# Moving the Gram matrices of a delta rule one group sooner, from key copies of their own, in a kernel that overlaps it with two feed-forward layers

## The chip, the cores and the metric

The kernel runs on one core of one Trainium2 chip. The metric is the device time of one execution in microseconds; the time of the kernel before is the median of three runs. One further execution was recorded by the hardware profiler, and everything that is read from "the trace" below is of that one. Engines: TensorE (PE in the rows; PEld is its weight load), VectorE (DVE), ScalarE (ACT), GpSimd (POOL) and SyncE (SP), which issues the DMAs. Each executes its own instructions in order.

## What is computed

```python
for t in range(S):                       # attention: B=4, H=8, S=768, D=48
    kt, vt, bt = k_n[:, :, t], v[:, :, t], beta[:, :, t, None]
    y[:, :, t] = einsum('bhd,bhde->bhe', q[:, :, t], state)
    v_old = einsum('bhde,bhd->bhe', state, kt)
    state = state + bt[..., None] * einsum('bhd,bhe->bhde', kt, vt - v_old)
x = y as 3072 tokens x 384
h = x @ w_in;  g = h if h >= 1, 0 if h <= -1, else (h + 1)**2 / 4;  x = g @ w_out   # 384 -> 2048 -> 384
h = x @ w_in2; r = max(h, 0);                                      out = (r * r) @ w_out2
```

The keys `k_n` are normalized rows of `k`. All is float32; the kernel forms each product of the feed-forward layers from a high and a low part of both factors, three matmuls for one.

## The kernel before

**Attention.** Time is cut into 24 chunks of 32 tokens. Within a chunk the recurrence becomes a triangular system, and its matrix comes from the Gram matrix of the chunk's keys. Chunks are taken in six groups of four. For a group, `gram` (TensorE, L272) makes the products of keys with keys and queries of a chunk, and VectorE masks them into `gp` (L284). `tri` inverts the triangles of a whole group: `begin` transposes `gp` to `gm` (VectorE, L325), a preparation of some ten small instructions normalizes (L238 to L355, the last large one L354), then 30 steps of two GpSimd instructions each (L370, L376) work on `tx`, and `end` transposes `tx` back into `gp` (VectorE, L380). Only then can the first chunk of the group use it. The inversions of groups 1 to 5 run on GpSimd; that of group 0 stands at the start, on VectorE and GpSimd together.

A chunk has six steps on TensorE: `ks` (keys with state, L406), `tr` (with the inverse, L420), `qs` (queries with state, `yy`, L406), `ku` (the state's update, `sps`, L451), `pu` (L440) and `xt` (transposes the result for the feed-forward, L474). `value` scales a chunk's keys on GpSimd (L249).

**Feed-forward.** Tokens go in nine blocks of two or three chunks in the first layer (256 or 384 columns), and in eight blocks of three in the second. A block has 16 units, one for each 128 rows of the hidden layer. A unit is nine `h` matmuls into PSUM, the activation, and two units later nine `acc` matmuls (all L489). In the first layer the activation is ScalarE's `r` and `g` (L514, L515), VectorE's clamp (L516), ScalarE's square (L517), VectorE's sum (L518), then the split of `g` into high (ScalarE, L526) and low part (VectorE, L527). There is one L518 for each unit of the first layer, so units are counted below by their L518.

**Order.** Attention runs one block ahead of the feed-forward that consumes it. A table maps half-units (slots) to steps: a list `todo` for each block holds the steps of its chunks and the Grams, spread evenly over 32 slots; `at[c]` is the slot in which chunk `c` begins, `ready[c]` that of its Gram. TensorE executes in the order written; for the other engines a list scheduler picks the order from a simulated timeline, unless `issue_after` ties an instruction to another. `later` ties to the last L514 and L516 (`marks`). Keys and queries of a chunk (`kqt`) lie in a ring of six buffers, values (`kv`) in one of three; the ring of `kqt` serves later for second-layer weights (`w2r`).

Of the kernel before, what the change touches and what calls it, by code (L numbers as in the profile page):

```python
# [8 lines left out]
F32 = mybir.dt.float32  # L9
# [12 lines left out]
GROUPS = [4] * 6  # L22
# [3 lines left out]
def kernel(  # L26
# [38 lines left out]
    LENT = 28  # L65
    RG = 3
    RAW = 3
    WT, WL = 3, 4
    GB = 2
    MANY = 4  # L70
# [31 lines left out]
    def att(shape, name):  # L102
        tag = "att"
        if turn[0] is not None:
            tag = early[turn[0] % len(early)]
            turn[0] += 1
        return ps.tile(shape, F32, tag=tag, bufs=2 if tag == "att" else 1, name=name)
# [6 lines left out]
    kqt, kvt, gp, nt, xh, xl = {}, {}, {}, {}, {}, {}  # L114


    def load_kq(c, tag="kqt", bufs=6):
        if c >= NCH:
            return
        t = kqt[c] = ring.tile([P, B2, H, 2 * T], F32, tag=tag, bufs=bufs, name="kqt")  # L120
        for o in range(2):
            nc.sync.dma_start(
                t[64 * o:64 * o + D].rearrange("p b h x -> p (b h x)"), kq[c, D * o:D * (o + 1)]
            )

    def load_kv(c):
        if c >= NCH:
# [87 lines left out]
    w2r = {}  # L215

    def fetch_w2(f):
        w2r[f] = ring.tile([P, 2, DM], F32, tag="kqt", bufs=6, name="w2r")
        nc.sync.dma_start(w2r[f], w2f[f])

    def place_w2(f):
# [33 lines left out]
    def per_bh(f):  # L255
        for h in range(H):
            for b in range(B):
                f(b, h, slice(T * b, T * (b + 1)), slice(64 * (b % 2), 64 * (b % 2) + D))

    def gram(c, lo=0, hi=2, late=0):  # L260


        n, j = group_of[c]
        if j == 0 and lo == 0:
            gp[n] = ring.tile([P, 2, GC, H, T], F32, tag="gp", bufs=2, name="gp")
            if GROUPS[n] < GC:
                nc.gpsimd.memset(gp[n][:, 0, GROUPS[n]:], 0.0)
        g = att([P, H, hi - lo, T], "g")

        def one_(b, h, p, pd):  # L270
            x = kqt[c][pd, b // 2, h]
            nc.tensor.matmul(  # L272
                g[p, h].rearrange("p x i -> p (x i)"), x[:, 0:T], x[:, lo * T:hi * T],
                start=h == 0, stop=True, skip_group_check=True,
            )

        per_bh(one_)

        dst = gp[n][:, lo:hi, j].rearrange("p x h i -> p h x i")
        if late > 1:  # L280
            nc.scalar.copy(dst, g)

        def keep():
            nc.vector.tensor_mul(  # L284
                dst,
                dst if late > 1 else g,
                mask[:, lo:hi].rearrange("p (o x) i -> p o x i", o=1)
                .to_broadcast([P, H, hi - lo, T]),
            )

        if late:
            return keep
        keep()
# [97 lines left out]
    def chunk_steps(c):  # L391
# [38 lines left out]
        def qs():  # L430
            o = t["o"] = att([P, H, D], "yy")
            of_state(o, 1)
            if c >= HEADS:
                kqt.pop(c)
                load_kq(c + 6)

        def pu():
            o = t["o"]
# [163 lines left out]
    w1f = flow(w1s)  # L602
    w1f.reverse()

    PACE = 6
    SPREAD = 3
    behind = [nullcontext]

# [6 lines left out]
    with tc.manual_schedule():  # L615
        for c in range(GC):
            load_kq(c)
        nc.sync.dma_start(bet, beta)
        first1()
        load_kq(4)  # L620
        load_kq(5)
        for c in range(3):
            load_kv(c)
        nc.gpsimd.memset(zero, 0.0)
        nc.gpsimd.memset(one, 1.0)
        nc.gpsimd.memset(tiny, 1e-36)
        nc.gpsimd.memset(neg1, -1.0)
        nc.scalar.activation(st[:, 0, 0, 0:1], one, AF.Sqrt, bias=zero)
        nc.gpsimd.memset(mask, 1.0)
        nc.gpsimd.memset(tx, 0.0)  # L630
        for b in range(B):
            for o, op in enumerate((ALU.is_ge, ALU.is_gt)):
                m_ = mask[T * b:T * (b + 1), o]
                nc.gpsimd.affine_select(
                    m_, m_, pattern=[[1, T]], compare_op=op, fill=0.0,
                    base=0, channel_multiplier=-1,
                )
        make_identity(nc, ident)
        for c in range(GROUPS[0]):
            gram(c, 0, 1)  # L640
        begin, pre, steps, end = tri(0, [(V, 0, 3), (V, 3, 9), (G, 9, T)])
        begin()
        go(pre[:1])
        masks = [gram(0, 1, 2, late=2)]
        cross_gram(0, 1)
        go(pre[1:])
        more_w1()
        masks += [gram(c, 1, 2, late=2) for c in range(1, GROUPS[0])]
        for c in range(HEADS):
            load_kq(c + 6)  # L650
        late = masks[HEADS:]
        masks[HEADS:] = [gram(c, late=1) for c in range(GFIRST[1], GFIRST[2])]
        go(steps)
        for c in range(3):
            value(c)
        ins = end()
        go(masks)
        behind[0] = lambda: tc.issue_after(ins.ins)
    ENGINES = {mybir.EngineType.PE}
    with tc.manual_schedule(engines=ENGINES):  # L660
# [15 lines left out]
        begin()  # L676
        go(pre)
        go(t1)
        end1()
        turn[0] = None  # L680

        SL = 2 * NF
# [2 lines left out]
        def put(n, slot, *fs):  # L685
            for i, f in enumerate(fs):
                exb.setdefault(SL * n + slot + i, []).append(f)

        def later(*fs):

            def one_(f):
                with tc.issue_after(marks[0].ins), tc.issue_after(marks[1].ins):
                    f()

            return [lambda f=f: one_(f) for f in fs]

        def put_a(n, slot, f):
            exa.setdefault(SL * n + slot, []).append(f)

        at, ready, due = {}, {}, [GFIRST[2]]
        for n in range(1, NB):
            todo = []
            for c in range(FIRST[n], FIRST[n] + SIZES[n]):
                left = {0: 1, 1: 1, 2: 0, 3: 2}[c % GC]
                for i, s_ in enumerate(chunk_steps(c)):
                    todo.append(((at, c) if i == 0 else None, s_))
                    x = due[0]
                    if i + left > 5 and x < NCH:  # L710
                        left -= 1
                        due[0] += 1
                        todo.append(((ready, x), lambda x=x: gram(x)))
            for i, (mark, s_) in enumerate(todo):
                o = 0 if n > 1 else HEAD
                slot = SL * (n - 1) + o + i * (SL - o) // len(todo)
                if mark:
                    mark[0][mark[1]] = slot
                put_a(0, slot, s_)
        for c in range(3, NCH):  # L720
            put(0, max(0, at[c] - 5), lambda c=c: value(c))

        def tri_put(g, a, z):
            begin, pre, steps, end = tri(g, [(G, 0, T)])
            begin()
            for i, s_ in enumerate(pre):
                put(0, a + i // 3, s_)
            a += 4
            for i, s_ in enumerate(steps):
                put(0, a + i * min(z - a, PACE) // len(steps), s_)  # L730
            put(0, z, end)

        for g in range(2, NG):
            a, z = ready[GFIRST[g] + GROUPS[g] - 1], at[GFIRST[g]]
# [99 lines left out]
```

## Time and profile before

| what | value |
|---|---|
| median of three runs | 1101.67 us (1101.43 to 1104.24) |
| the profiled execution | 1103.17 us |
| its span in the trace | 1101.1 us |
| TensorE busy | 995.3 us, 90% of the span |
| VectorE, ScalarE, GpSimd busy | 609.3, 506.4, 293.1 us |
| mean granted clock of TensorE | 0.963 of full |

The span is the time between the first and the last instruction that the profiler recorded; what lies around it is 2.1 us in this execution. A busy share says little where matmuls are pipelined; gaps and waits say more. The first layer ends at about 700 us of the span.

### The profile page before, as it was taken

To read this page: it belongs to the slowest core of one execution; us is meant where nothing else is said; L and a number is where in the kernel's file an instruction comes from. 1 tells how busy PE (TensorE), PEld (TensorE's weight loads), DVE (VectorE), ACT (ScalarE), POOL (GpSimd) and SP (SyncE) were. 2 spreads that over 40 slices of the span, in tenths; PEclk is the share of its full clock that TensorE was granted. 3 is DMA by queue.
4 is the path that set the end of the run, shared out by engine and by line. 5 is a ranking of instruction groups with operands and counts; after the bars stand their busy time and mean duration, and the time that the engine had idled before them with its cause. 6 is when DMAs were issued, how large, how long until landed. Compare 5 with 4: busy or idle time off the path is not lost.

```text
span 1101.1 us, 32911 instructions
## 1 busy us (share of the span) xinstructions
PE 995.3 (90%) x14312; PEld 952.0 (86%) x14312; DVE 609.3 (55%) x1187; ACT 506.4 (46%) x1068; POOL 293.1 (27%) x446
## 2 busy tenths in 40 slices
PE   4345799969997997999799999899999999999998
PEld 3335699969986997899699999899999999999998
DVE  4998566754764583557644467744434343434333
ACT  1065466535544653555455666433333333333332
POOL 3467600850391058007600022310101010101000
PEclk9966899989998999899899999999999999999999
DMA  8065145223331340231211122201001010000000
GB/s 235 33 209 165 35 131 158 82 80 88 89 103 52 96 132 30 81 118 31 74 31 52 32 87 87 72 1 44 22 23 43 1 43 1 22 1 22 1 22 22
DMA packets 33488, 72.99 MB, mean 66 GB/s; under 512 B 3904, under 2 KB 17728, under 8 KB 33344
## 3 DMA queue, kind: packets, MB, share of 16 engines
q1 hardware_dynamic: 33344, 70.89, 20.9%
q8 instruction: 112, 1.84, 0.7%
q14 instruction: 32, 0.26, 0.1%
HBM read 55.15 MB, written 15.73 MB: 64 GB/s over the span
## 4 chain that ended last, share of the span: by engine, by line
PE 64%; POOL 15%; DVE 11%; issue 4%; ACT 3%; DMA 1%; SPq 0%; DVEq 0%; POOLq 0%; ACTq 0%
PE h L489 29%; PE acc L489 29%; POOL tx L376 7%; POOL t L370 7%; DVE g L518 1%; PE g L272 1%; DVE t L370 1%; DVE tx L376 1%; DVE wl L161 1%; PE tr L420 1%; PE yy L406 1%; DVE wl L164 1%; PE ks L406 1%; PE yy L440 1%; PE sps L451 1%
## 5 line engine op out<-in xcount | busy, mean ns | idle before, releaser
L489 PE MATMUL h<-xh,w 128*128 128x384 f32 (+1 forms) x1632 | 325.8, 336 | 31.3 <-ACT g L515 28.2
L489 PEld LDWEIGHTS h<-xh,w 128*128 128x128 f32 x1632 | 276.7, 193 | 37.5 <-ACT g L515 27.8
L527 DVE TENSOR_TENSOR gl<-g,gh 128x384 fp32r<-128x384 f32 (+1 forms) x272 | 167.2, 615 | 133.3 <-ACT gh L526 128.5
L526 ACT CAST gh<-g 128x384 fp32r<-128x384 f32 (+1 forms) x272 | 134.5, 494 | 209.7 <-DVE g L518 107.8
L489 PE MATMUL h<-xl,w 128*128 128x384 f32 (+1 forms) x816 | 181.3, 331 | 0.0
L489 PE MATMUL acc<-gh,w 128*128 128x384 f32 (+1 forms) x864 | 170.3, 333 | 7.2 <-ACT gh L526 6.5
L521 DVE TENSOR_TENSOR g<-r 128x384 f32<-128x384 f32 x128 | 71.3, 557 | 157.7 <-ACT r L520 157.7
L489 PE MATMUL acc<-w,gh 128*128 128x384 f32 x768 | 155.6, 337 | 1.6 <-DVE e L534 1.6
L520 ACT ACTIVATE r<-h,zero 128x384 f32<-128x384 f32 x128 | 74.5, 582 | 166.4 <-PE h L489 166.4
L489 PEld LDWEIGHTS acc<-gh,w 128*128 128x128 f32 x864 | 139.1, 193 | 12.7 <-ACT gh L526 6.6
L489 PEld LDWEIGHTS h<-xl,w 128*128 128x128 f32 x816 | 143.4, 193 | 0.0
L489 PEld LDWEIGHTS acc<-w,gh 128*128 128x128 f32 x768 | 136.3, 188 | 1.9 <-ACT gh L526 1.9
L514 ACT ACTIVATE r<-h,one 128x384 f32<-128x384 f32 (+1 forms) x144 | 78.4, 544 | 84.7 <-PE h L489 83.2
L518 DVE TENSOR_TENSOR g<-g,r 128x384 f32<-128x384 f32 (+1 forms) x144 | 89.0, 618 | 39.5 <-ACT r L517 38.2
L516 DVE TENSOR_SCALAR r<-r 128x384 f32<-128x384 f32 (+1 forms) x144 | 60.4, 419 | 84.9 <-ACT r L514 84.7
L376 POOL TENSOR_TENSOR tx<-tx,t 128x30 f32<-128x30 f32 (+16 forms) x171 | 95.5, 559 | 12.8
L370 POOL TENSOR_TENSOR t<-tx,gm 128x30 f32<-128x30 f32 (+16 forms) x171 | 92.7, 542 | 17.2 <-DVE tx L354 4.7
L489 PE MATMUL acc<-gl,w 128*128 128x384 f32 (+1 forms) x432 | 91.9, 322 | 2.3 <-DVE gl L527 2.3
L517 ACT ACTIVATE r<-r 128x384 f32<-128x384 f32 (+1 forms) x144 | 70.5, 490 | 49.5 <-DVE r L516 48.7
L249 POOL TENSOR_TENSOR kv<-kv,nt 128x384 f32<-128x384 f32 x24 | 21.7, 905 | 267.7 <-DMA kv<-in_kv_dram 73.2
L489 PE MATMUL acc<-w,gl 128*128 128x384 f32 x384 | 88.0, 337 | 0.0
L576 POOL CAST xh<-x2r 128x1152 fp32r<-128x1152 f32 x8 | 9.5, 1187 | 293.2 <-PE h L489 293.2
(85 smaller groups left out, 968.6 us busy)
## 6 DMA issues: line engine op xcount, KB each, us to landing
raw<-in_w_dram SPq DMA_DIRECT2D x64, 384.0 KB, 3.7
kqt<-in_kq_dram SPq DMA_DIRECT2D x48, 192.0 KB, 3.8
kv<-in_kv_dram SPq DMA_DIRECT2D x24, 384.0 KB, 3.1
w2f<-wl SPq DMA_DIRECT2D x32, 192.0 KB, 3.6
w2r<-w2f SPq DMA_DIRECT2D x16, 384.0 KB, 3.0
x2r<-x SPq DMA_DIRECT2D x8, 576.0 KB, 4.2
out_dram<-e SPq DMA_DIRECT2D x24, 192.0 KB, 1.9
x<-e SPq DMA_DIRECT2D x18, 192.0 KB, 3.4
```

The lines of the kernel that those rows point to most:

```text
L370: eng.tensor_mul(t, x[:, lo:hi, j:j + 1].to_broadcast([P, hi - lo, w]), gm[:, j:j + 1, j + 1:T].to_broadcast([P, hi - lo, w]),)
L376: ins = eng.tensor_add(x[:, lo:hi, j + 1:T], x[:, lo:hi, j + 1:T], t)
L406: per_bh(lambda b, h, p, pd: nc.tensor.matmul(o[p, h], kqt[c][pd, b // 2, h, x * T:(x + 1) * T], st[pd, b // 2, h], start=h == 0, stop=x = ...
L489: nc.tensor.matmul(o, *((r, l) if swap else (l, r)), **flags)
L514: marks[0] = nc.scalar.activation(r, h, AF.Relu, bias=one)
L516: marks[1] = nc.vector.tensor_scalar(r, r, 2.0, 0.5, ALU.min, ALU.mult)
L517: nc.scalar.activation(r, r, AF.Square)
L518: nc.vector.tensor_add(g, g, r)
L520: marks[0] = nc.scalar.activation(r, h, AF.Relu, bias=zero)
L521: marks[1] = nc.vector.tensor_mul(g, r, r)
L526: nc.scalar.copy(ghi, g)
L527: nc.vector.tensor_sub(glo, g, ghi.bitcast(F32))
```

## The change

Five edits go together. The keys and queries are loaded a second time for the Grams of chunks 4 to 23, into a ring of their own with two buffers (`kqg`); the ring `kqt` shrinks from six buffers to four. The four Grams of a group are all put into the first chunk of the group before it, one behind each of its steps 1 to 4, where they were spread over its last three chunks and the next group's first. The 30 inversion steps are spread over the slots up to four before the group is needed, where they were put into at most six slots. The transposition back of groups 2 to 5 is put one slot sooner and goes through `later`. That of group 1, which stood right behind its steps before the units began, is put two slots ahead of chunk 4, also through `later`.

```diff
+    KQ, KG = 4, 2
...
+    def load_kg(c):
+        if c < NCH and c not in kqg:
+            kqg[c] = fetch_kq(c, "kqg", KG)
...
-        w2r[f] = ring.tile([P, 2, DM], F32, tag="kqt", bufs=6, name="w2r")
+        w2r[f] = ring.tile([P, 2, DM], F32, tag="kqt", bufs=KQ, name="w2r")
...
+        src = kqt[c] if c < KQ else kqg[c]
...
         per_bh(one_)
+        if c >= KQ:
+            kqg.pop(c)
+            load_kg(c + KG)
...
                 kqt.pop(c)
-                load_kq(c + 6)
+                load_kq(c + KQ)
...
-        load_kq(4)
-        load_kq(5)
+        for c in range(KG):
+            load_kg(KQ + c)
...
         go(t1)
-        end1()
         turn[0] = None
...
-                left = {0: 1, 1: 1, 2: 0, 3: 2}[c % GC]
+                g, j = group_of[c]
+                due = []
+                if j == 0 and 1 <= g < NG - 1:
+                    due = list(range(GFIRST[g + 1], GFIRST[g + 1] + GROUPS[g + 1]))
                 for i, s_ in enumerate(chunk_steps(c)):
                     todo.append(((at, c) if i == 0 else None, s_))
-                    x = due[0]
-                    if i + left > 5 and x < NCH:
-                        left -= 1
-                        due[0] += 1
+                    if i and due:
+                        x = due.pop(0)
                         todo.append(((ready, x), lambda x=x: gram(x)))
...
+        put(0, at[GFIRST[1]] - 2, *later(end1))
...
-            a += 4
+            a += 3
             for i, s_ in enumerate(steps):
-                put(0, a + i * min(z - a, PACE) // len(steps), s_)
-            put(0, z, end)
+                put(0, a + i * (z - 4 - a) // len(steps), s_)
+            put(0, z - 1, *later(end))
```

What this makes of VectorE's order is shown at three places. In the changed kernel the same instructions stand on other lines: L516, L518 and L527 are L531, L533 and L542; L284, L325 and L380 are L299, L340 and L395; L477 and L416 are L492 and L431; L161 and L164 are L172 and L175.

The first place is where group 2 begins: the mask of its last Gram and the transposition of `gp`. On VectorE before, from the 27th unit sum on:

```order
L518 TENSOR_TENSOR g<-g,r 128x256
L284 TENSOR_TENSOR gp<-g,mask 128x8x2x32
L325 STREAM_TRANSPOSE gm<-gp 128x32x32
L527 TENSOR_TENSOR gl<-g,gh 128x256
L516 TENSOR_SCALAR r<-r 128x256
```

On VectorE of the changed kernel, from the 22nd unit sum on:

```order
L533 TENSOR_TENSOR g<-g,r 128x256
L542 TENSOR_TENSOR gl<-g,gh 128x256
L299 TENSOR_TENSOR gp<-g,mask 128x8x2x32
L340 STREAM_TRANSPOSE gm<-gp 128x32x32
L531 TENSOR_SCALAR r<-r 128x256
```

The beginning of group 2 moved five units to the front (groups 3, 4 and 5 likewise, by 5 to 6 units). L354 moved from just behind the 29th sum to just ahead of the 25th.

The second place is where group 2 ends: the transposition back. On VectorE before, from the 36th unit sum to the next:

```order
L518 TENSOR_TENSOR g<-g,r 128x384
L284 TENSOR_TENSOR gp<-g,mask 128x8x2x32
L527 TENSOR_TENSOR gl<-g,gh 128x384
L516 TENSOR_SCALAR r<-r 128x384
L161 TENSOR_SCALAR wl<-raw 128x384
L164 SCALAR_TENSOR_TENSOR wl<-wt,wl 128x384
L477 TENSOR_TENSOR xl<-xt,xh 128x3x128
L380 STREAM_TRANSPOSE gp<-tx 128x32x32
L518 TENSOR_TENSOR g<-g,r 128x384
```

On VectorE of the changed kernel, from the 35th unit sum to the next:

```order
L533 TENSOR_TENSOR g<-g,r 128x384
L542 TENSOR_TENSOR gl<-g,gh 128x384
L531 TENSOR_SCALAR r<-r 128x384
L395 STREAM_TRANSPOSE gp<-tx 128x32x32
L533 TENSOR_TENSOR g<-g,r 128x384
```

The transposition moved one unit to the front, and stands directly behind the clamp of a unit. The other groups' transpositions stand behind the 56th, 78th and 100th sum before, and behind the 56th, 79th and 103rd now; L354 stood behind the 49th, 70th and 92nd, and stands behind the 44th, 65th and 88th.

The third place is the transposition back of group 1. On VectorE before, from the 8th unit sum to the next:

```order
L518 TENSOR_TENSOR g<-g,r 128x256
L527 TENSOR_TENSOR gl<-g,gh 128x256
L380 STREAM_TRANSPOSE gp<-tx 128x32x32
L516 TENSOR_SCALAR r<-r 128x256
L477 TENSOR_TENSOR xl<-xt,xh 128x3x128
L518 TENSOR_TENSOR g<-g,r 128x256
```

On VectorE of the changed kernel, from the 15th unit sum to the next:

```order
L533 TENSOR_TENSOR g<-g,r 128x256
L542 TENSOR_TENSOR gl<-g,gh 128x256
L531 TENSOR_SCALAR r<-r 128x256
L395 STREAM_TRANSPOSE gp<-tx 128x32x32
L492 TENSOR_TENSOR xl<-xt,xh 128x3x128
L533 TENSOR_TENSOR g<-g,r 128x256
```

It moved seven units to the back, and from ahead of a unit's clamp to behind it.

## Rows read from the trace of the kernel before

**Rows 1.** The page: TensorE's busy time, and its granted clock in 40 slices.

```profile
PE 995.3 (90%) x14312; PEld 952.0 (86%) x14312; DVE 609.3 (55%) x1187; ACT 506.4 (46%) x1068; POOL 293.1 (27%) x446
...
PEclk9966899989998999899899999999999999999999
```

**Rows 2.** The list of waits: who waited for whom, total us, times, longest.

```profile
DVE gp L380 <- POOL tx L376: 40.0, 5, 9.7
...
PE h L489 <- ACT g L515: 28.2, 7, 8.4
...
PE tr L420 <- DVE gp L380: 12.1, 1, 12.1
```

**Rows 3.** Timeline of TensorE at its five restarts: start, us, [idle before, releaser].

```profile
131.20 1.65 PE L489 MATMUL h<-xh,w 128*128 128x256 f32 x6 [6.99 <-ACT g L515]
...
240.78 2.29 PE L489 MATMUL h<-xh,w 128*128 128x384 f32 x6 [8.36 <-ACT g L515]
...
337.86 1.93 PE L272 MATMUL g<-kqt 48*32 48x64 f32 x64 [7.65 <-DVE gp L284]
...
442.40 1.93 PE L272 MATMUL g<-kqt 48*32 48x64 f32 x64 [7.69 <-DVE gp L284]
...
548.63 2.29 PE L489 MATMUL h<-xh,w 128*128 128x384 f32 x6 [6.43 <-ACT g L515]
```

**Rows 4.** Chain of waits, 180 to 250 us (group 2): start, us, what.

```profile
187.22 1.03 PE g L272 x64
...
197.42 0.69 DVE tx L354
198.18 0.38 POOL t L370
...
212.47 0.79 POOL kv L249
...
236.94 0.27 POOL tx L376
...
240.78 3.25 PE h L489 x9
...
245.75 0.81 PE tr L420 x64
246.56 1.76 PE h L489 x9
```

**Rows 5.** Chain of waits behind the gaps of groups 4 and 5.

```profile
444.33 3.18 PE acc L489 x9
447.50 2.32 PE h L489 x9
...
551.88 2.88 PE acc L489 x9
```

**Rows 6.** Timeline of VectorE: the 25th and 36th L518, three transpositions back.

```profile
182.50 0.42 DVE L518 TENSOR_TENSOR g<-g,r 128x256 f32<-128x256 f32 x1
...
224.12 1.04 DVE L518 TENSOR_TENSOR g<-g,r 128x384 f32<-128x384 f32 x1 [0.59 <-ACT r L517]
...
237.23 2.06 DVE L380 STREAM_TRANSPOSE gp<-tx 128x1024 f32<-128x1024 f32 x1 [7.83 <-POOL tx L376]
...
334.71 2.01 DVE L380 STREAM_TRANSPOSE gp<-tx 128x1024 f32<-128x1024 f32 x1 [9.65 <-POOL tx L376]
...
543.65 2.00 DVE L380 STREAM_TRANSPOSE gp<-tx 128x1024 f32<-128x1024 f32 x1 [6.44 <-POOL tx L376]
```

**Rows 7.** Chain of waits: the 18th step from the end, groups 3 and 5.

```profile
325.60 0.59 POOL t L370
...
534.09 0.59 POOL t L370
```

**Rows 8.** Busy time by engine: PE, PEld, DVE, ACT, POOL, then clock, DMA, GB/s.

```profile
130.00:140.00 10.00, 8.80 (x224) 8.13 (x228) 8.66 (x20) 7.59 (x21) 2.33 (x3) 0.75 0.31 99
```

**Rows 9.** DMA issues: KB each, median us from issue to landing.

```profile
kqt<-in_kq_dram SPq DMA_DIRECT2D x48, 192.0 KB, 3.8
```

More of the change, by code (lines that the diff above doesn't have):

```diff
@@ L114, with load_kq, fetch_kq @@
     kqt, kvt, gp, nt, xh, xl = {}, {}, {}, {}, {}, {}
[L117 to L120, printed above, removed]
+    def load_kq(c):
+        if c < NCH:
+            kqt[c] = fetch_kq(c, "kqt", KQ)
+    kqg = {}
+    def load_kg(c):
+        if c < NCH and c not in kqg:
+            kqg[c] = fetch_kq(c, "kqg", KG)
+    def fetch_kq(c, tag, bufs):
+        t = ring.tile([P, B2, H, 2 * T], F32, tag=tag, bufs=bufs, name="kqt")
         for o in range(2):
@@ L124, in load_kq @@
             )
+        return t
     def load_kv(c):
@@ L268, in gram @@
         g = att([P, H, hi - lo, T], "g")
+        src = kqt[c] if c < KQ else kqg[c]
         def one_(b, h, p, pd):
-            x = kqt[c][pd, b // 2, h]
+            x = src[pd, b // 2, h]
             nc.tensor.matmul(
@@ L603 @@
     w1f.reverse()
-    PACE = 6
     SPREAD = 3
@@ L649 @@
         for c in range(HEADS):
-            load_kq(c + 6)
+            load_kq(c + KQ)
         late = masks[HEADS:]
@@ L698, in put_a @@
             exa.setdefault(SL * n + slot, []).append(f)
-        at, ready, due = {}, {}, [GFIRST[2]]
+        at, ready = {}, {}
         for n in range(1, NB):
@@ L705 @@
             for c in range(FIRST[n], FIRST[n] + SIZES[n]):
-                left = {0: 1, 1: 1, 2: 0, 3: 2}[c % GC]
+                g, j = group_of[c]
+                due = []
+                if j == 0 and 1 <= g < NG - 1:
+                    due = list(range(GFIRST[g + 1], GFIRST[g + 1] + GROUPS[g + 1]))
                 for i, s_ in enumerate(chunk_steps(c)):
                     todo.append(((at, c) if i == 0 else None, s_))
-                    x = due[0]
-                    if i + left > 5 and x < NCH:
-                        left -= 1
-                        due[0] += 1
+                    if i and due:
+                        x = due.pop(0)
                         todo.append(((ready, x), lambda x=x: gram(x)))
+                assert not due
             for i, (mark, s_) in enumerate(todo):
```

## The prediction

> **What bounds the kernel now.** The page comes first: TensorE is busy for 90% of the span, and its granted clock sits at full speed except in three slices near the start and in four single slices behind them [rows 1]. So the kernel is TensorE-bound wherever TensorE runs, and what can be won is idle time and slow clock. The list of waits says who idles: one line, the transposition of the inverted triangles on VectorE, waited 40.0 us in five pieces for GpSimd's inversion steps, and TensorE waited 28.2 us in `h` for ScalarE's `g` [rows 2]. VectorE's own timeline shows three of the five transpositions (groups 2, 3 and 5): idle 7.83, 9.65 and 6.44 us in front of each, then some 2.0 us of work [rows 6]. TensorE's timeline has a gap beside each: 6.99, 8.36, 7.65, 7.69 and 6.43 us for groups 1 to 5, 37.1 us in sum [rows 3]. The link is VectorE's in-order queue. The transposition stands in it in front of feed-forward instructions (L516, L518); while it waits, those wait, ScalarE's `g` can't be overwritten and the next `h` can't start. The chain of waits of group 2 shows it whole: L354 at 197.42, GpSimd steps from 198.18 to 237.21 with one key scaling (0.79) among them, and `h` again at 240.78 [rows 4]. GpSimd needs 39 us; VectorE came to the transposition 32 us behind L354 (237.23 - 7.83 = 229.4) [rows 4, 6].
>
> The gap has a second price: behind it TensorE runs slow, at the lower of its two levels. Nine `h` matmuls take 3.25 us right behind the gap and 1.76 at 246.56 [rows 4]. I price it by the rows: group 2, 1.49; group 3, a Gram of 1.93 against 1.03, and one `h` as in group 2, 2.39; group 4, a Gram again, 3.18 and 2.32 against 1.76, 2.88; group 5, one `h`, and 2.88 against 1.76, 2.61 [rows 3 to 5]; group 1, with 256 columns where the others have 384, two thirds of 1.49, 1.0. Together 10.4 us. The five gaps thus cost 37.1 + 10.4 = 47.5 us, and this is all that I let the change win.
>
> **The change, part by part.** *Grams sooner.* The four Grams of a group are issued in the first chunk of the group before it. The order puts the last `gm` transposition of group 2 behind the 22nd L518 instead of the 27th, and its way back behind the 35th instead of the 36th. L354 moves from the 29th to just ahead of the 25th. Is GpSimd then in time? In the trace, the 25th L518 starts at 182.50 and the 36th at 224.12: 41.6 us [rows 6]. In that stretch the new order has one Gram less (1.03) and three chunk steps more (0.81 each, as `tr`) [rows 4]: 43.0. The transposition stands half a us ahead of the 36th L518: ready 42.5 us behind the 25th. GpSimd starts some 0.7 us behind the 25th L518 (L355 stands between), takes 39.0, and now has two key scalings in its queue instead of one, 0.79 more [rows 4]. It has also to run beside a working VectorE at its end, where VectorE stood idle until now. The last 18 steps took 9.1 us from 325.60 in group 3, VectorE idle throughout, and 9.6 from 534.09 in group 5, where it still worked for the first 3 us (543.65 - 6.44 = 537.2) [rows 6, 7]: 0.4 for each 3 us, so 1.2 for the stretch. Sum 0.7 + 39.0 + 0.8 + 1.2 = 41.7 against 42.5: just in time, with nothing to spare. If it is late, the first 2 us or so cost nothing, because L516 of the unit now stands ahead of it and TensorE still has a unit of `acc` and `h` queued. I take 1.0 us for group 2, bounds 0 and its whole 9.9 (8.36 + 1.49).
>
> Groups 3, 4 and 5 get 12, 14 and 15 units between L354 and the transposition, where they had 7, 8 and 8. In group 3 the chain ended at 334.71 and VectorE was ready 9.65 us sooner [rows 6], so with a chain of about 40 us seven units took some 30, 4.3 each; twelve and more are 52, 60 and 65 us for a chain of 41. These gaps go, with over 10 us to spare.
>
> The Trainium skill (SBUF — State Buffer, "Who interferes with whom") says that a VectorE instruction with two SBUF inputs and a GpSimd instruction that reads SBUF lock each other out of a shared port, the second one fully. The trace agrees in direction (the 0.4 us above). This speaks against the change: the chain will have a working VectorE beside it to its end. That this could be worse than 1.2 us is a rival below.
>
> *Group 1's transposition* goes from behind the 8th L518 to behind the 15th; GpSimd ended where VectorE's wait did, seven units sooner, so there is no wait left. What is late next there is VectorE itself: in the 10 us around the restart it was busy for 8.66 with first-layer weights [rows 8], and that work now has to fit beside a TensorE that doesn't pause. Bounds: nothing, or the whole 8.0 of this gap; I take 1.5, since 8.66 of 10 leaves little but isn't over.
>
> *Queued behind a feed-forward unit.* The transposition still takes 2.0 us of VectorE, now behind L516. ScalarE's square of that unit and TensorE's queued `acc` and `h` cover it; without this cover it would cost up to 2.0 us each, 10 in all.
>
> *Steps spread.* GpSimd executes in order and has nothing else to do but key scalings; the spread changes their place among the steps, no duration. A scaling waits in the middle of the chain for its values' DMA, and the steps behind it with it. For group 2 the values of chunk 8 can load when chunk 5 is transposed, behind the 27th `h`; at 3.8 us a unit (41.6 / 11) that is some 8 us into the chain, and the scaling comes 14 us into it (212.47 - 198.18) [rows 4, 6]; a landing is 3.8 us at the keys' [rows 9]. Nothing, by 2 to 3 us.
>
> *Key copies of their own.* Twenty chunks are loaded twice, 40 DMAs of 192 KB more on SP's queue. TensorE waits for one only if it lands later than the Gram two places on: six half-units, some 11 us, against 3.8 [rows 6, 9]. In the queue, weight loads and stores of the same units stand ahead of them; each waits for something of about the same place. At the start the loads for Grams 6 to 9 wait for Grams 4 to 7, two landings in a row; TensorE has 12.1 us of idle time there [rows 2]. With this cover gone: 3.8 us once. The shorter ring (4 for 6) loads a chunk's keys four chunks ahead, and second-layer weights nine half-units ahead: nothing.
>
> *Crowding.* Four Grams and a preparation now fall in the narrow (256-column) second block, and next to each other in the later ones; VectorE masks each Gram. I take 0.5 us for each of groups 3 to 5, bounds 0 and 3.
>
> **The sum.** 47.5 - 1.5 (group 1) - 1.0 (group 2) - 1.5 (groups 3 to 5) = 43.5 us. The profiled execution took 1103.17 (span 1101.1): 1059.7. The median of the runs is 1101.67, 1.5 below it: **1058**.
>
> **Rivals.** *New waits keep part of it.* VectorE becomes the limit around the preparations, and group 2 (the only one without slack) stays late. For: VectorE's 8.66 of 10 us, and a sum for group 2 within 1 us. Against: in the old preparation stretches TensorE had no gap. If each of the five keeps 4 us, 20 in all, 1078; between 1066 and 1090.
>
> *The port rule in full.* If each of the last 18 steps loses a VectorE instruction of 0.42 us [rows 6], the chain of group 2 is 7.6 longer than now instead of 1.2: 5.6 late. A wait of 7.83 left a gap of 8.36, so about 6 us of gap and 1.5 of slow clock come back: 1066 less the 1.0 already taken, 1065. The other groups have the slack for it. The measured 0.4 us in 3 speaks for less. By the rule of the Trainium skill (SBUF — State Buffer) on full blocking this rival is the outcome.
>
> *The change doesn't do what it says:* the transposition waits as long at its new place, because GpSimd's start moves with it. Then 1102, within 0.3%, which is about what a measurement of this kernel can tell from no change. The order speaks against it: 11 to 15 units instead of 7 or 8.
>
> *Slower: keys come late.* A Gram that waits for its keys stops TensorE, with a slow clock behind. This decides once a load takes more than about 11 us instead of 3.8 from the Gram that frees its buffer, because SP stands at a weight load ahead of it; the sixteen Grams must each lose over 43.5 / 16 = 2.7 us for the time to pass the old one. At 3.5 each, 56 us on 1058: 1114. The trace can't exclude it, since keys came six chunks ahead so far.
>
> **Chances.** All five gaps gone, 1050 to 1066: 0.68, the port rule's 1065 in it with 0.1. Part kept, 1066 to 1090: 0.23. No change: 0.03. Slower: 0.04. Better than 1050: 0.02. Range 1050 to 1077: the first case and half of the second, 8 in 10. Faster by over 0.3%: 0.93; same: 0.03; slower: 0.04.
>
> **What would show it.** VectorE's wait for GpSimd at the transposition falls from 40.0 us to under 4; TensorE's five gaps are gone and PEclk is full from slice 6 or so on; GpSimd's chain takes 40 to 42 us and no key scaling in it waits for a DMA; the second layer (behind 700 us) keeps its length. It is wrong if TensorE shows waits for `kqt` above 1 us in the first layer, if a transposition still waits over 4 us, or if TensorE's gaps reappear in front of `g` or `h` behind VectorE's preparation.

## The result and the profile after

The changed kernel takes **1068.35 us** (median of 4 runs, 1067.42 to 1069.27) against 1101.72 of the kernel before beside it: ratio 0.9692, 95% interval 0.9675 to 0.9710. That is 33.4 us less. The forecast was 1058 (43.5 us less) in a range of 1050 to 1077. The direction and the range hold; some 10 us of the gain are missing.

The page of the kernel after, TensorE's busy time and the granted clock in 40 slices, which answer to [rows 1]:

```profile
PE 987.0 (92%) x14312; PEld 942.3 (88%) x14312; DVE 611.7 (57%) x1187; ACT 505.5 (47%) x1068; POOL 300.3 (28%) x446
...
PEclk9967899999999999999999999999999999999999
```

The single slow slices behind the start are gone. The lists of waits of VectorE and TensorE (total us, times, longest) answer to [rows 2]:

```profile
DVE wl L172 <- POOL w L190: 4.4, 2, 3.9
DVE gp L395 <- POOL tx L391: 2.6, 1, 2.6
...
PE tr L435 <- DVE kv L431: 11.2, 5, 5.1
PE h L504 <- ACT g L530: 9.2, 6, 3.3
```

The wait of the transposition (now L395) fell from 40.0 us in five pieces to 2.6 in one, in group 2. A line that was not among the large ones (0.4 us before) is new: a weight conversion (L172) waits for GpSimd's L190, the low part of a first-layer weight.

TensorE's timeline at its restarts in the first layer (start, us, what, [idle before, releaser]) answers to [rows 3], where five gaps of 6.4 to 8.4 us stood:

```profile
107.19 0.98 PE L504 MATMUL acc<-gh,w 128*128 128x256 f32 x6
...
125.31 0.97 PE L504 MATMUL h<-xh,w 128*128 128x256 f32 x6 [1.84 <-ACT g L530]
...
131.77 1.50 PE L435 MATMUL tr<-kv,gp 32*32 32x48 f32 x64 [5.14 <-DVE kv L431]
133.20 1.65 PE L504 MATMUL acc<-gh,w 128*128 128x256 f32 x6
...
228.62 1.42 PE L504 MATMUL h<-xh,w 128*128 128x384 f32 x6 [1.96 <-ACT g L530]
...
323.32 0.88 PE L435 MATMUL tr<-kv,gp 32*32 32x48 f32 x64 [1.33 <-DVE kv L431]
```

Groups 3 to 5 have nothing above 1.4 us left. Group 2 keeps a gap of 1.96. Around group 1's old gap there are two, 7.0 us in sum, with slow clock behind the second (133.20: 1.65 us for what took 0.98 at 107.19; the granted clock from 130 to 140 us is 0.62). So "TensorE's five gaps are gone" holds for groups 3 to 5 alone.

Where the gain came from is seen by the start of the same L518 (now L533) in both kernels, at units by which TensorE has executed the same Grams and, but for one `ku` at the 77th, the same chunk steps in both:

| unit | before, us | after, us | gained so far | gained in the group | forecast |
|---|---|---|---|---|---|
| 35 (group 1) | 220.62 | 219.49 | 1.1 | 1.1 | 8.0 - 1.5 = 6.5 |
| 50 (group 2) | 296.48 | 290.08 | 6.4 | 5.3 | 9.9 - 1.0 = 8.9 |
| 77 (group 3) | 423.79 | 409.04 | 14.8 | 8.4 | 10.0 - 0.5 = 9.5 |
| 100 (group 4) | 534.82 | 509.72 | 25.1 | 10.3 | 10.6 - 0.5 = 10.1 |
| 120 (group 5) | 614.37 | 580.56 | 33.8 | 8.7 | 9.0 - 0.5 = 8.5 |

Groups 3 to 5 came out as forecast, 27.4 against 28.1. Of the missing 9 to 10 us, 9.0 are in group 1 (5.4) and group 2 (3.6). The second layer kept its length: from the 144th unit to the end 408.3 us in both.

In group 1, VectorE's timeline, and under it GpSimd's, show what stands there instead:

```profile
124.70 0.35 DVE L172 TENSOR_SCALAR wl<-raw 128x384 int32<-128x384 uint32 x1
128.99 0.97 DVE L172 TENSOR_SCALAR wl<-raw 128x384 int32<-128x384 uint32 x1 [3.95 <-POOL w L190]
129.88 1.37 DVE L190 TENSOR_TENSOR w<-wl,w 128x384 fp32r<-128x384 f32 x1
131.17 0.54 DVE L431 TENSOR_TENSOR kv<-kv,ks 128x384 f32<-128x384 f32 x1
```

```profile
127.75 0.26 POOL L391 TENSOR_TENSOR tx<-tx,t 128x30 f32<-128x30 f32 x1
127.97 0.99 POOL L190 TENSOR_TENSOR w<-wl,w 128x384 fp32r<-128x384 f32 x1
```

The last step of the chain (127.75) is followed by a low part (L190), and VectorE's next L172 needs the `wl` buffer that it frees. VectorE stands from 125.0 to 129.0 behind the same chain as before, by another instruction; `kv` (131.17), for which TensorE waits, stands behind it.

In group 2, preparation and transposition on VectorE, and under them both ends of the chain on GpSimd:

```profile
182.78 0.68 DVE L369 TENSOR_TENSOR tx<-gm,st 128x512 f32<-128x512 f32 x1
...
183.85 0.46 DVE L533 TENSOR_TENSOR g<-g,r 128x256 f32<-128x256 f32 x1
...
224.47 2.18 DVE L395 STREAM_TRANSPOSE gp<-tx 128x1024 f32<-128x1024 f32 x1 [2.58 <-POOL tx L391]
```

```profile
183.54 0.49 POOL L385 TENSOR_TENSOR t<-tx,gm 128x30 f32<-128x30 f32 x1 [1.10 <-DVE tx L369]
...
224.18 0.27 POOL L391 TENSOR_TENSOR tx<-tx,t 128x30 f32<-128x30 f32 x1
```

The chain took 224.45 - 183.54 = 40.9 us, as worked out (39.0 + 0.8 + 1.2 = 41.0). Those of groups 3 to 5 took 40.9, 41.6 and 41.2 us, and no key scaling waits for a DMA within any of the four. VectorE was ready at 224.47 - 2.58 = 221.89, which is 38.0 behind the 25th unit (183.85) and not 42.5.

### The profile page after: what moved, and what is told of

The parts are those of the page before. It is cut to its first block, busy times and chain, and to the rows that moved or that the text cites. A ratio compares the mean times of both kernels' runs of the same rounds, so it can differ in the third digit from the quotient of the medians.

```text
span 1067.3 us, 32978 instructions
## 1 busy us (share of the span) xinstructions
PE 987.0 (92%) x14312; PEld 942.3 (88%) x14312; DVE 611.7 (57%) x1187; ACT 505.5 (47%) x1068; POOL 300.3 (28%) x446
## 4 chain that ended last, share of the span: by engine, by line
PE 72%; DVE 6%; POOL 3%; ACT 3%; issue 2%; DMA 0%; DVEq 0%; ACTq 0%; POOLq 0%
PE acc L504 32%; PE h L504 32%; DVE g L533 2%; POOL tx L391 2%; POOL t L385 2%; PE tr L435 1%; PE yy L421 1%; PE g L284 1%; PE yy L455 1%; PE sps L466 1%; ACT r L529 1%; PE ks L421 1%; DVE gl L542 1%; ACT g L530 1%; DVE r L531 1%
## 5 line engine op out<-in xcount | busy, mean ns | idle before, releaser
L504 PE MATMUL h<-xh,w 128*128 128x384 f32 (+1 forms) x1632 | 320.8, 332 | 12.4 <-ACT g L530 9.2
L504 PEld LDWEIGHTS h<-xh,w 128*128 128x128 f32 x1632 | 272.8, 190 | 18.3 <-ACT g L530 9.0
L542 DVE TENSOR_TENSOR gl<-g,gh 128x384 fp32r<-128x384 f32 (+1 forms) x272 | 168.4, 619 | 134.5 <-ACT gh L541 131.2
L504 PEld LDWEIGHTS acc<-gh,w 128*128 128x128 f32 x864 | 136.8, 190 | 12.4 <-ACT gh L541 7.1
L533 DVE TENSOR_TENSOR g<-g,r 128x384 f32<-128x384 f32 (+1 forms) x144 | 89.7, 623 | 40.6 <-ACT r L532 39.4
L531 DVE TENSOR_SCALAR r<-r 128x384 f32<-128x384 f32 (+1 forms) x144 | 64.7, 449 | 80.4 <-ACT r L529 79.8
L391 POOL TENSOR_TENSOR tx<-tx,t 128x30 f32<-128x30 f32 (+16 forms) x171 | 98.5, 576 | 12.7
L385 POOL TENSOR_TENSOR t<-tx,gm 128x30 f32<-128x30 f32 (+16 forms) x171 | 95.3, 557 | 17.7 <-DVE tx L369 5.2
L530 ACT ACTIVATE g<-h,neg 128x384 f32<-128x384 f32 (+1 forms) x144 | 77.6, 539 | 0.0
```

Of the source, the lines that this page charges most:

```text
L385: eng.tensor_mul(t, x[:, lo:hi, j:j + 1].to_broadcast([P, hi - lo, w]), gm[:, j:j + 1, j + 1:T].to_broadcast([P, hi - lo, w]),)
L391: ins = eng.tensor_add(x[:, lo:hi, j + 1:T], x[:, lo:hi, j + 1:T], t)
L504: nc.tensor.matmul(o, *((r, l) if swap else (l, r)), **flags)
L530: nc.scalar.activation(g, h, AF.Relu, bias=neg1)
L531: marks[1] = nc.vector.tensor_scalar(r, r, 2.0, 0.5, ALU.min, ALU.mult)
L533: nc.vector.tensor_add(g, g, r)
```

## The experiments

Each group of four ran on one chip with the kernel before beside it; the ratio is that to the kernel before.

| run | median, us | ratio, 95% interval |
|---|---|---|
| the changed kernel | 1068.35 | 0.9692 [0.9675, 0.9710] |
| 1, group 1's transposition at its old place | 1073.89 | 0.9735 [0.9719, 0.9751] |
| 2, three low parts on VectorE | 1066.85 | 0.9673 [0.9659, 0.9688] |
| 3, Grams sooner alone | 1108.33 | 1.0050 [1.0035, 1.0065] |
| 4, later place alone | 1079.90 | 0.9792 [0.9778, 0.9807] |
| 5, two Grams behind a step | 1069.69 | 0.9703 [0.9687, 0.9720] |
| 6, as 2, conversions even | 1064.44 | 0.9652 [0.9630, 0.9675] |
| 7, keys loaded twice | 1086.10 | 0.9847 [0.9824, 0.9869] |
| 8, as 6 and 5 | 1065.53 | 0.9662 [0.9648, 0.9677] |
| 9, group 2's transposition a unit later | 1064.90 | 0.9649 [0.9632, 0.9665] |
| 10, no inversion of group 1 | 1057.35 | 0.9586 [0.9571, 0.9600] |
| 11, conversions even, and 9 | 1062.25 | 0.9632 [0.9618, 0.9647] |
| 12, as 6 and 9 | **1060.78** | 0.9613 [0.9599, 0.9627] |

**1. Is group 1's new place worth anything?**

```diff
+        end1()
         turn[0] = None
...
-        put(0, at[GFIRST[1]] - 2, *later(end1))
```

> The changed kernel with one part undone: the transposition back of group 1 stands behind the 8th L518 again, as before, instead of the 15th. Theory A (group 1's wait only changed its place): in the changed kernel the transposition does not wait any more, but a weight conversion on VectorE (L172) waits 3.95 us for GpSimd's L190, which is queued behind the same inversion chain, and the units behind it are where they were in the kernel before; so the old place costs nothing: 1067 to 1070 us. Rival B (the prediction's term): the new place of group 1 is worth its 6.5 us and the missing 10 us lie elsewhere: 1075 us.

1073.89, close to B: theory A falls, the new place is worth 0.43%, 4.7 us. The transposition at its old place waits longer than in the kernel before, and TensorE with it (the two timelines of this run):

```profile
126.82 2.01 DVE L395 STREAM_TRANSPOSE gp<-tx 128x1024 f32<-128x1024 f32 x1 [11.66 <-POOL tx L391]
```

```profile
130.65 0.90 PE L489 MATMUL xt<-ident,kv 128*128 128x128 f32 x3 [11.07 <-ACT kv L459]
```

TensorE restarts when it did (130.65 against 131.20 [rows 3]), but it stood from 119.6 us on, where it worked until 124.2 before: in the new order it had less to execute ahead of the chain's end. VectorE came to the transposition sooner, at 126.82 - 11.66 = 115.16, and only waited longer for the same chain. At the 35th unit this kernel is at 225.00, 4.4 us behind the kernel before. So the new order of chunk steps and Grams, with the transposition still at its old place, costs group 1's stretch 4.4 us, the later place wins 5.5 (219.49), and 1.1 is left. The prediction had the second of the two and not the first.

**2. Does the wait of L172 hold the stretch?**

```diff
-            (nc.vector if i else nc.gpsimd).tensor_sub(lo, box["t"], hi.bitcast(F32))
+            (nc.vector if i or f > 12 else nc.gpsimd).tensor_sub(lo, box["t"], hi.bitcast(F32))
```

> The changed kernel with the low parts of the last three first-layer weights that GpSimd makes (L190, 1.0 to 1.2 us each, queued behind the inversion of group 1) made by VectorE instead, as it makes the other half of them (0.55 us each, 1.7 us more on VectorE). Theory A (VectorE waits there for GpSimd's L190 to free its buffer): the 3.95 us wait of L172 goes, TensorE's gaps of 1.84 and 5.14 us at 125 to 132 us shrink to under 2 in sum, and with the slow clock behind them 5 to 7 us are won: 1061 to 1064 us. Rival B (VectorE is full there anyway, and the L190 was only named for something else that is late): no gain, 1068 us or 1 to 2 us more.

1066.85, 0.19% or 2.1 us less: between the two, and with intervals that overlap. The wait is gone (0.4 us are left) and the 11th unit starts at 129.40 instead of 132.91, 3.5 us sooner. But TensorE keeps two gaps, 4.1 us in sum where there were 7.0, and by the 35th unit 2.0 us are left of the 3.5 (217.49 against 219.49):

```profile
126.26 0.97 PE L504 MATMUL h<-xh,w 128*128 128x256 f32 x6 [2.61 <-ACT g L530]
...
131.62 1.65 PE L504 MATMUL h<-xh,w 128*128 128x256 f32 x6 [1.46 <-ACT g L530]
```

**3 and 4. Which part of the change carries the gain?** Run 3 has the Grams of the changed kernel with the old pace and the old end of all groups, group 1's as in run 1. Run 4 is the kernel before with the new pace and the new end of groups 2 to 5. The edit of run 3 against the changed kernel, without the lines of run 1 (run 4 makes the reverse of it in the kernel before):

```diff
-            a += 3
+            a += 4
...
-                put(0, a + i * (z - 4 - a) // len(steps), s_)
-            put(0, z - 1, *later(end))
+                put(0, a + i * min(z - a, 6) // len(steps), s_)
+            put(0, z, end)
```

> The Grams of the changed kernel (one group sooner, from their own key copies) with the old rest: steps at the old pace, the transpositions back not tied behind a feed-forward unit, group 1 at its old place. The order then has the transposition 9, 7, 8 and 7 units behind the preparation in groups 2 to 5 (before 7, 7, 8, 8; changed kernel 11, 12, 14, 15). Theory A (the distance in units between preparation and transposition decides, 4.3 us a unit against a chain of 40 us): only group 2 wins, some 8 us, and group 5 loses 4: 1094 to 1100 us. Rival B (Grams sooner carry the gain wherever the transposition stands): under 1075 us.

> The kernel before with one part of the change alone: steps spread and the transpositions back of groups 2 to 5 tied behind a feed-forward unit; Grams at their old places, keys from the old ring, group 1 as before. The order then has the transposition 8, 9, 9 and 11 units behind the preparation (before 7, 7, 8, 8). Theory A (distance in units decides): the waits of 7.83, 9.65, 9.66 and 6.44 us fall to about 4, 1, 5 and 0, and some slow clock with them, but the transposition now ends shortly before TensorE needs it, which may give back 1 to 2 us a group: 1072 to 1082 us. Rival B (a wait on the same chain only moves with the instruction): 1098 to 1102 us.

Run 3 is 0.5% slower than the kernel before, worse than A's forecast (1094 to 1100) and far from B's. Run 4 wins 23.2 us, as A had it, though group 2's transposition still waits 7.07 us, where A had 4. VectorE's timeline of run 3, groups 2 and 5, and of run 4, groups 2 and 3:

```profile
188.13 0.68 DVE L369 TENSOR_TENSOR tx<-gm,st 128x512 f32<-128x512 f32 x1
...
227.90 2.07 DVE L395 STREAM_TRANSPOSE gp<-tx 128x1024 f32<-128x1024 f32 x1 [8.98 <-POOL tx L391]
...
530.00 2.06 DVE L395 STREAM_TRANSPOSE gp<-tx 128x1024 f32<-128x1024 f32 x1 [10.29 <-POOL tx L391]
```

```profile
197.64 0.68 DVE L354 TENSOR_TENSOR tx<-gm,st 128x512 f32<-128x512 f32 x1
...
238.31 2.04 DVE L380 STREAM_TRANSPOSE gp<-tx 128x1024 f32<-128x1024 f32 x1 [7.07 <-POOL tx L376]
...
292.89 1.11 DVE L354 TENSOR_TENSOR tx<-gm,st 128x512 f32<-128x512 f32 x1
...
335.54 2.19 DVE L380 STREAM_TRANSPOSE gp<-tx 128x1024 f32<-128x1024 f32 x1 [1.24 <-POOL tx L376]
```

The wait is the chain's time, from the preparation's last large instruction to the transposition (39.8 to 42.7 us here), less the time from the preparation to the point where VectorE is ready. In run 3's group 2 that time is 227.90 - 8.98 - 188.13 = 30.8 us for 9 units (39.8 - 30.8 = 9.0 of wait); in run 4's groups 2 and 3 it is 33.6 and 41.4; in the changed kernel's group 2, 39.1. Grams sooner alone win nothing, because a transposition that is not tied goes up with them in the order (9, 7, 8 and 7 units behind the preparation). A had counted units of 4.3 us; the narrow units (256 columns) of group 2 lasted 3.4.

**5 and 8. Can group 2 be mended by Grams still sooner?**

```diff
-                    if i and due:
-                        x = due.pop(0)
+                    for x in due[:2] if i else ():
+                        due.pop(0)
```

> The changed kernel with two Grams behind one chunk step instead of one, so that a group's four Grams and its preparation come one to two units sooner still: the order has the transposition 13 units behind the preparation in group 2 (11 in the changed kernel) and 14, 17 and 17 in groups 3 to 5. Theory A (group 2 is late because its 11 units last only 39.1 us from L369 to the point where VectorE is ready, against a chain of 41.7 us; 13 units are some 45): its wait of 2.58 us and TensorE's gap of 1.96 us go, with the slow clock behind it: 2 to 3.5 us won, 1065 to 1067 us. Rival B (Grams side by side crowd VectorE's masks and the PSUM buffers): 1068 to 1072 us, with new gaps in front of g.

> All three edits together on the changed kernel: last three low parts on VectorE, conversions even from unit 3 on, two Grams behind one step. Theory A (group 1's stretch by VectorE's rush, group 2 by its distance; the two are apart in time and add up): 1056 to 1061 us. Rival B (one takes what the other gives, as in the second run, where 3.5 us won by unit 11 were 1.5 by unit 40, since group 2's chain starts and ends by its own Grams): 1062 to 1066 us.

Run 5 gives no gain, 1069.69: B in size. Its transposition in group 2 does not wait, but TensorE loses the same elsewhere, in small pieces at group 2's Grams (0.28 at 165, 0.52 at 167, 0.27 and 0.34 at 173 and 179 us) and one at group 3's:

```profile
258.82 0.55 PE L489 MATMUL xt<-ident,kv 128*128 128x128 f32 x3 [1.68 <-ACT kv L459]
```

By the 100th unit both kernels are at the same place (509.73 and 509.72). Run 8 is run 6 with this edit, and 0.1% above it, inside the intervals: B again.

**9. Can it be mended by one unit more?**

```diff
-            put(0, z - 1, *later(end))
+            put(0, z + 1 if g == 2 else z - 1, *later(end))
```

> The changed kernel with group 2's transposition back one unit later (behind the 36th L518 instead of the 35th); nothing else moves. Theory A (group 2 is late by 2.58 us because its distance is 39.1 us and its chain 41.7; a unit is 3.5 to 4 us, and TensorE needs the result some two units later): the wait goes, TensorE's gap of 1.96 us and the slow clock behind it shrink to under 1 us: 1065.5 to 1067.5 us. Rival B (TensorE then waits for the transposition itself in front of tr, as in the kernel with the later place alone): 1068 to 1071 us.

1064.90, 0.43% or 4.7 us less than the changed kernel by the ratios, 3.6 by the profiled spans (1067.3 and 1063.7): A. The order moves one row; VectorE comes to it after the chain's end:

```profile
182.01 0.68 DVE L369 TENSOR_TENSOR tx<-gm,st 128x512 f32<-128x512 f32 x1
...
224.63 2.23 DVE L395 STREAM_TRANSPOSE gp<-tx 128x1024 f32<-128x1024 f32 x1
```

From the 35th to the 50th unit it takes 67.17 us instead of 70.59; of these 3.4 us 0.6 are given back by the 77th, and 0.8 of the spans' 3.6 were won ahead of the 35th, where the order is the same. So group 2's lateness cost about 3 us: a gap of 1.96 and the slow clock behind it (granted clock 0.50 from 230 to 232 us, the lower level).

**6. Is VectorE's rush what is left of group 1's stretch?** On the kernel of run 2:

```diff
-                    put(n, i, *(later(more_w1) if i > SL // 2 + 1 else [more_w1]))
+                    put(n, i, *(later(more_w1) if i > 5 else [more_w1]))
```

> The kernel of the second run (last three low parts on VectorE) with first-layer weight conversions tied one behind each half-unit from unit 3 on instead of from unit 9 on, so that VectorE converts evenly instead of in two rushes (it is busy for 20.0 of 20 us from 80 to 100 us, 5.3 of 10 from 110 to 120, 8.95 of 10 from 130 to 140 in the changed kernel). Theory A (what is left of group 1's stretch is VectorE's rush, not the chain): the units 1 to 12 get shorter and the gaps at 126 and 132 us go: 4 to 8 us under the second run, 1059 to 1063 us. Rival B (weights come later and TensorE or GpSimd's L190 wait for them, or the total of VectorE's work sets the stretch): 1065 us or more.

1064.44, 0.21% or 2.3 us under run 2 by the ratios, with intervals that overlap (4.5 by the profiled spans, 1060.0 and 1064.5): less than A by the medians. The first units come up to 16 us sooner (the third at 81.82 instead of 98.00 in run 2), but all but 0.8 us of this is gone by the eighth (113.74 and 114.52). Busy time by engine (PE, PEld, DVE, ACT, POOL, clock, DMA share, GB/s) of run 6 shows VectorE nearly full there all the time, which is the second half of B:

```profile
90.00:100.00 10.00, 8.96 (x188) 8.25 (x179) 10.00 (x14) 5.67 (x15) 9.61 (x12) 0.80 0.30 96
100.00:110.00 10.00, 5.88 (x90) 4.99 (x88) 8.95 (x15) 4.72 (x12) 7.63 (x10) 0.83 0.67 196
110.00:120.00 10.00, 6.90 (x102) 6.30 (x103) 9.47 (x16) 6.73 (x17) 8.07 (x11) 0.90 0.41 124
120.00:130.00 10.00, 8.94 (x167) 7.69 (x165) 9.73 (x22) 7.03 (x18) 5.68 (x12) 0.76 0.44 155
```

**10. What does the chain of group 1 still cost?** The inversion of this group is left out but for its first step:

```diff
-        go(t1)
+        go(t1[:1])
```

> The changed kernel without the inversion steps of group 1 but the first (GpSimd's L385 and L391 from 70 to 128 us, 35 us of work, are left out, so the triangles of group 1 are not inverted); all the rest stands. It shows what the chain costs its stretch now that the transposition does not wait for it. Theory A (the chain still holds group 1's stretch, through the low parts queued behind it and by slowing VectorE's instructions beside it): by the 16th unit 8 us or more are won, and VectorE's L175 takes 0.55 us each instead of up to 1.37: 1056 to 1061 us. Rival B (the stretch is set by VectorE's own work and the weights' loads, GpSimd costs it nothing but the 3.95 us): 1063 to 1066 us.

1057.35: A in time. At the 16th unit 12.8 us are won (137.40 against 150.17): 6.8 by the fourth unit, where VectorE converts in a rush beside GpSimd, and 4.7 between the tenth and the eleventh, where L172 waited. The part of A on L175 was wrong (up to 1.37 us here too); another instruction shows it. L531 from 70 to 130 us, min/median/max ns, in the changed kernel and then in this one:

```profile
L531 DVE TENSOR_SCALAR r<-r x11: 279/543/1097, 80.3 to 124.2; 128x256 f32<-128x256 f32 x11
```

```profile
L531 DVE TENSOR_SCALAR r<-r x14: 278/293/887, 79.0 to 128.6; 128x256 f32<-128x256 f32 x14
```

**7. Are the extra key loads free?**

```diff
+            if tag == "kqg":
+                nc.sync.dma_start(
+                    t[64 * o:64 * o + D].rearrange("p b h x -> p (b h x)"), kq[c, D * o:D * (o + 1)]
+                )
```

> The changed kernel with each of the extra key copies loaded twice (40 more DMAs of 192 KB on SP's queue, into the same buffer). Theory A (the prediction's: the extra loads cost nothing, since a Gram has 11 us for a load of 3.5): within 1 us of the changed kernel, 1067 to 1070 us, and no wait for the keys in the first layer behind 60 us. Rival B (the loads are part of the missing 10 us): each Gram stands longer, 16 of them by 0.3 us or more: 1073 us or more.

1086.10, 17 us more by the ratios: B in size, but not in place. 12.8 us are lost before the first unit (97.10 against 84.34), of which 3 are won back by the 11th; some 8 more are lost between the 19th and the 26th unit, at group 2's Grams, and none behind that (16.6 at the 50th unit, 16.1 at the 100th). The second load writes where the first does, and SP's queue stands for it. SP's own waits of this run from 165 to 210 us:

```profile
SPq L136 <- DMA kqt<-in_kq_dram: 15.0, 7, 4.1
SPq L161 <- DVE wl L176: 8.5, 1, 8.5
```

That is the rival on late keys, made to happen: SP stands, and Grams wait (two by 0.56 and 2.33 us there; where the rest of the 8 us comes from is not shown). In the changed kernel itself TensorE waits for keys only ahead of 40 us (8.1 us), where the chain of group 0 sets the time: its first transposition is used at 48.63 us, at 48.47 before.

**11 and 12. What the three edits give together.** Run 12 is run 6 with the edit of run 9; run 11 is the same with the last low parts left on GpSimd.

> The changed kernel with conversions even from unit 3 on and group 2's transposition a unit later; the last low parts stay on GpSimd. Theory A (evenly placed low parts do not stand behind the whole chain any more, so they need not go to VectorE, which is full here): 1058 to 1062 us, under the next kernel. Rival B (GpSimd's low parts, in its queue between the steps, hold up VectorE's conversions through their buffers): 1063 us or more.

> The same with the last three low parts on VectorE as well: the sixth run with group 2's transposition a unit later. Theory A (the two edits are apart in time and add up): 1 to 3 us under the sixth run, 1060 to 1063 us by medians. Rival B (group 2's chain starts late by its own Grams, so an earlier start of the stretch does not help and the later place delays tr): no gain, 1064 us or more.

Run 12 is the fastest that leaves nothing out, 1060.78: 0.8% under the changed kernel, 3.9% under the one before. The edits of groups 1 and 2 add up. Run 11 at 0.9632 is 0.2% above it, with intervals that overlap: whether low parts on VectorE help here is not shown either way.

## Why the prediction was right and wrong

**What bounds the kernel, and the price of a gap: right.** Groups 3 to 5 gave back 27.4 us where 29.6 were to be had and 28.1 were forecast, so the gaps and the slow clock behind them were rightly found and sized there. In group 2, run 9 brings the stretch from the 35th to the 50th unit from 75.86 us before to 67.17, 8.7 of the 9.9 that were to be had.

**Steps spread: right, for a simpler reason.** With the old pace put back, the order of instructions on all five engines is the same row by row, so this edit changes nothing.

**Queued behind a feed-forward unit: undervalued.** I priced it as two us of cover each. Run 3 shows that it is what holds the transposition where it is; without it the Grams' lead is lost. The order that I read held it, so the sum did not suffer.

**Group 1, "there is no wait left", 1.5 us: this step failed.** The transposition did not wait, but I looked only at that instruction, and not at what else stands in GpSimd's queue behind the same chain. A low part stands there, and VectorE's conversions wait for its buffer: 3.5 us at the 11th unit and 2.0 at the 35th by run 2. The sum also had no term for the new order of chunk steps, which leaves TensorE less to execute ahead of the chain's end and costs 4.4 us while the transposition is at its old place (run 1). The rest is the crowding that I named (8.66 of 10 us busy) and held for small; how the three share the loss at the new place is not shown. The bound was right (the whole 8.0; 6.9 were lost), the value taken from it was not. The chain costs this stretch more than its gap: without it, run 10 wins 12.8 us more.

**Group 2, "ready 42.5 us behind the 25th", 1.0 us: this step failed by its second number.** The chain was right to 0.1 us. But VectorE was ready 38.0 us behind the 25th sum. Run 9, where the transposition is out of the way, shows the 11 units by themselves: 183.09 to 222.08, 39.0 us, where I had worked out 43.0. TensorE has no gap in this stretch, nor in that of the kernel before, so the difference is matmuls. The kernel before executes two Grams there (187.22 [rows 4], and the first of group 3 behind a step of chunk 7), and the new order none; I took off one, 1.0 us too little:

```profile
222.49 1.10 PE L272 MATMUL g<-kqt 48*32 48x64 f32 x64
```

(The section on the change has the old Grams too late: two of a group stood in the last chunk of the group two before, the others in the first two chunks of the group before.) The new order has two chunk steps more, a `ku` and an `xt`, 1.1 us, and I added three, 2.4. And the preparation now stands on VectorE ahead of the 25th sum, so that TensorE has executed `h` for 26 units by then where it had for 25: one `h` of 256 columns, 1.2 us. That is 3.5 of the 4.0 us. The transposition also stands 1.0 us ahead of the 36th sum, not half a us. The cover that I counted on ("the first 2 us or so cost nothing") was not there: 2.58 us late left a gap of 1.96 and cost about 3, by run 9.

**Crowding in groups 3 to 5, 1.5 us: about right** (29.6 - 27.4 = 2.2 lost). **Keys: right at this rate,** and with less to spare in group 2 than "11 us against 3.8" says (run 7).

**The rivals.** The outcome is the one called "new waits keep part of it" (1066 to 1090, 0.23): group 2 late and VectorE the limit, as it said, but in two groups and not in five. The likeliest case, all gaps gone, did not come. *The port rule in full* did not either: the chain took 40.9 us, not the 47.4 that it needs (39.0 + 0.8 + 7.6). The last 18 GpSimd instructions (nine steps of two; the prediction calls them 18 steps) took 224.45 - 212.89 - 1.14 for the scaling between them = 10.4 us, 1.3 more than the 9.1 of [rows 6, 7]. The Trainium skill (SBUF — State Buffer, "Who interferes with whom") also says that a tensor_scalar of VectorE can take the shared port pair, when its operands meet the conditions for it. What this makes of VectorE was not in the forecast. L531 in run 10 agrees with it: its median is 0.29 us without most of the chain and 0.54 beside it.

## What to carry to other kernels

When an instruction is taken out of the way of a slow chain, list everything else that waits for an instruction queued behind that chain, through buffers too: the next one in line takes the wait over. A distance counted in units should be priced by the units that it will hold after the change, and where the sum comes out "just in time", one unit more (run 9, about 3 us won) did better than starting the chain sooner (run 5, nothing). Parts of a change may be worth -23 and +5 us alone (runs 4 and 3) and -29 together (run 1), so each is priced by the distance that it leaves, not by itself.

## What the runs showed of the hardware

Two of VectorE's instructions with all inputs in SBUF slow beside a working GpSimd: L531 (a tensor_scalar, one input) and L533 (two inputs). In the changed kernel, 384 columns each, min/median/max ns: L531 and L533 from 225 to 260 us, GpSimd almost idle (one scaling), and then from 266 to 306.5, beside the chain of group 3:

```profile
L531 DVE TENSOR_SCALAR r<-r x7: 359/360/360, 228.1 to 256.1; 128x384 f32<-128x384 f32 x7
```

```profile
L533 DVE TENSOR_TENSOR g<-g,r x8: 528/548/560, 226.5 to 257.1; 128x384 f32<-128x384 f32 x8
```

```profile
L531 DVE TENSOR_SCALAR r<-r x10: 347/628/809, 266.2 to 304.7; 128x384 f32<-128x384 f32 x10
```

```profile
L533 DVE TENSOR_TENSOR g<-g,r x10: 542/736/1071, 267.1 to 306.1; 128x384 f32<-128x384 f32 x10
```

The medians go from 0.36 to 0.63 us and from 0.55 to 0.74. Beside the chain of group 1 L533, with 256 columns there, hardly changed (median 0.425 us, 0.422 without most of the chain in run 10), while L531 did. L431 and L492, which have one of their two inputs in PSUM, took 0.52 to 0.57 us from 70 us on, beside every chain and away from it. Of run 10's 12.8 us, 6.8 were won ahead of the place where L172 waited, where VectorE was full. How much of these is slower VectorE instructions, and how much low parts between GpSimd's steps, the runs do not tell apart.
